# Down projection of an S5 scan plus GeGLU kernel: the h parts of more tiles ahead of the state parts in blocks 1 and 3, and other DMA numbers in its scheduler

## The chip, the cores and the metric

The kernel runs on one core of one Trainium2 chip. The metric is the device time of one execution in microseconds (us), a median over several executions. TensorE (PE in the profile) does the matmuls, VectorE (DVE) the element-wise work and the scans, ScalarE (ACT) activations and copies, GpSimd (POOL) a few small operations, and SyncE (SP) issues most of the transfers. Most executions of a kernel agree within 0.3%. The "granted clock" of a run is the mean share of full speed at which TensorE was clocked.

## The reference

The inputs are one sequence of 2048 rows with 512 columns, in bf16. Two branches read the same layer-normed rows, and the result is their sum plus the input.

```python
def _A_ref(x, ...):                       # S5: a complex diagonal state space
    Bu = jnp.einsum("bld,pd->blp", x + 0j, B_bar)
    for t in range(L):
        h = Lam_bar[None, :] * h + Bu[:, t, :]
    ...
    return 2.0 * jnp.einsum("blp,dp->bld", hseq, Cmat).real + x * Dskip

def _B_ref(x, w_gate, w_up, w_down):      # GeGLU, 512 -> 1376 -> 512
    return (_gelu(x @ w_gate) * (x @ w_up)) @ w_down

xn = _layernorm(x)
return x + _A_ref(xn, ...) + _B_ref(xn, ...)
```

The hidden product of the second branch is called h below, and the states of the first are called states. Both end in a matmul that adds to the same output tile.

## The kernel before

The rows are cut in four blocks (0 to 3) of 512 rows, each of four tiles of 128 rows. The program records every operation with what it reads and writes; a list scheduler then orders VectorE's, ScalarE's and GpSimd's work by estimated durations. TensorE and the DMA queue of SyncE keep the order in which the operations were recorded.

The estimate of a transfer is a number in one line. It places the transfer in the scheduler's mind and nothing else; a factor on the byte count stands for slow patterns:

```python
INORDER = ("tensor", "sync")
...
def dma(self, fn, nbytes, ..., queue="sync", issue=DMA_ISSUE):
    op = self._add(queue, fn, 2000.0 + nbytes / 0.30e3, "dma", reads, writes, tag, after)   # ns
...
def TR(b):                                # rows of block b, transposed, for TensorE
    for j, tt in enumerate(tts):
        S.dma(lambda e, ...: e.dma_start_transpose(XNT[b].ap[:, :, 128*j:128*(j+1)], XN[tt % 8].ap),
              3.0 * 128 * 1024, reads=[XN[tt % 8]], writes=[XTk[b][j]], tag="tr_x%d" % b, issue=1280.0)
```

The scan chain of a block runs on VectorE: four products and sums that rotate the inputs, eight scans, and four more that rotate back. The last of these (the line of the profile is L783) makes the states ready.

```python
def CHAIN(b, step=KP):
    ...
    V(... e.tensor_tensor_scan(g.ap, rb, g.ap, init, ALU.mult, ALU.add) ..., "scan")        # L767, 8 of them
    ...
    V(... e.tensor_tensor(TA.ap, ssb.ap, cos4, ALU.mult) ..., "post_c")                     # L779
    V(... e.tensor_tensor(TB.ap, ssb.ap, sin4, ALU.mult) ..., "post_s")                     # L780
    V(... e.tensor_tensor(ssb.ap[:, :, 0, :], TA..., TB..., ALU.add) ..., "post_re")        # L781
    V(... e.tensor_tensor(ssb.ap[:, :, 1, :], TB..., TA..., ALU.subtract) ..., "post_im")   # L783
```

The down projection DN(b) makes four output tiles. For each one, `seed` puts the input rows in a PSUM bank (where TensorE's sums are built up), `hidden` adds 11 matmuls over h, `states` adds 8 matmuls over the states, and `store` adds the skip term (L882) and stores the tile. The order of these on TensorE has three forms:

```python
def DN(b, split=False, tail=None):
    ...
    if split:
        for j in range(4):
            seed(j); hidden(j)
        for j in range(4):
            states(j); store(j)
    elif tail:
        for j in range(2):
            seed(j); hidden(j)
        for j in range(2):
            states(j); store(j)
        seed(2); hidden(2); states(2); store(2)
        parts = ((0, tail), (tail, D))    # the last tile in two column parts
        for c in parts:
            seed(3, *c)
        for c in parts:
            hidden(3, *c); states(3, *c); store(3, *c)
    else:
        for j in range(4):
            seed(j); hidden(j); states(j); store(j)
```

The end of the program's main part, where GU is the gate and up projection and BU the input projection of the states:

```python
        BU(2)
        CHAIN(2)
        DN(0, True)
        LN(3); SKIP(3)
        GU(2, [0, 1, 2, 10, 3, 4, 5, 6, 7]); TR(3); GU(2, [8, 9])
        BU(3)
        CHAIN(3)
        DN(1)
        GU(3, [0, 1, 2, 10, 3, 4, 5, 6, 7, 8, 9])
        DN(2)
        DN(3, tail=384)
```

## Time and profile before

| | before |
|---|---|
| time, median of 3 runs | 178.35 us (178.27 to 178.82) |
| profiled span | 176.6 us |
| TensorE's first and last matmul | from 1.02 to 174.1 us |
| states of block 1 ready / needed by TensorE | 106.6 / 108.4 us |
| states of block 3 ready / needed by TensorE | 160.9 / 162.2 us |

The first lines are from the page of the kernel before. The first gives the busy time of each engine with its share of the span and its count of instructions, the second the granted clock in 40 slices of the span.

```profile
PE 172.3 (98%) x873; PEld 84.5 (48%) x888; DVE 160.7 (91%) x283; ACT 89.5 (51%) x169; POOL 11.4 (6%) x25
...
PEclk9999999999999999999999999999999999999999
```

Two engines look full. Which one sets the time is read from the chain of work that ended last, followed back from the end and shown in order of time (start, length, what):

```profile
109.28 10.75 PE PS L864 x49
120.02 0.05 issue
120.08 2.54 PE PS L864 x11
122.62 5.18 PE PS L823 x24
127.80 1.32 PE PS L797 x16
129.12 0.05 issue
129.17 10.74 PE PS L823 x49
...
161.57 12.54 PE PS L864 x76
174.11 0.02 issue
174.13 0.29 DVE arena L882
```

It is TensorE from its first matmul on, and the only pauses are "issue" of 0.05 us. Even these are an artifact. The page counts 888 weight loads but only 873 matmuls. At 14 of the 15 such places the distance between two recorded starts is 0.432 us, exactly two matmuls of 128x512, and at the other, after a narrower one, it is 0.298 us, one narrow and one wide: one record is missing each time. Counting it, 50 matmuls of 128x512 take 10.79 us, or 215.8 ns each. The Trainium skill ("TensorE: Matmul & The Clock Gate", section "Wait — 56ns, not 53.3ns?") gives 215.7 ns from start to start once the clock is warm, and this trace agrees. So TensorE issues at its floor, with no gap, from about 6 us to the end. (The first seven matmuls, up to 3.98 us, stand 0.40 to 0.43 us apart, about half that rate, although the line PEclk has a 9 from the first slice on.)

VectorE in the timeline of the kernel before, at the start and the end of the chain of block 1 (L754, L783) and at the last chain (start, length, engine, line, operation, output and input, count, and in brackets what ended an idle time before it):

```profile
78.54 2.29 DVE L754 TENSOR_TENSOR arena<-arena 128x4096 bf16<-128x4096 bf16 x1
80.74 1.28 DVE L882 TENSOR_TENSOR arena<-PS,arena 128x512 bf16<-128x512 f32 x2
...
105.35 1.22 DVE L783 TENSOR_TENSOR arena<-arena 128x2048 bf16<-128x2048 bf16 x1
...
144.25 9.52 DVE L767 TENSOR_TENSOR_SCAN arena<-arena 128x512 bf16<-128x512 f32 x8
...
158.52 1.23 DVE L781 TENSOR_TENSOR arena<-arena 128x2048 bf16<-128x2048 bf16 x1
159.66 1.22 DVE L783 TENSOR_TENSOR arena<-arena 128x2048 bf16<-128x2048 bf16 x1
```

The chain of block 1 starts while two output adds of block 0 (L882) are still to come. The last chain ends at 159.66 + 1.22 = 160.9 us. TensorE wants these states at 162.2, found by counting the remaining matmuls back from the last one.

### The profile page before, as it was taken

The page shows a single profiled execution, that of the slowest core. Times are in us where ns is not written, and L with a number is a line of the kernel's source. Part 1 is how long each engine was busy: PE and PEld are TensorE (multiplying, and loading weights), DVE is VectorE, ACT ScalarE, POOL GpSimd, SP SyncE. Part 2 cuts the span into 40 slices and gives each one's busy share as a digit, 9 for nine tenths or more (in the row PEclk, how much of TensorE's full clock was granted, in tenths as well). Part 3 has the DMA queues.
Part 4 walks back from the last instruction along what each step waited for, and adds up shares of the span by engine and source line. Part 5 has one row for each costly group of instructions (what it writes and reads, how often), then busy time and mean ns, then how long its engine had stood idle before and what let it go on. Part 6 is the DMA issues. An engine that isn't in the chain of part 4 may idle for free.

```text
span 176.6 us, 2492 instructions
## 1 busy us (share of the span) xinstructions
PE 172.3 (98%) x873; PEld 84.5 (48%) x888; DVE 160.7 (91%) x283; ACT 89.5 (51%) x169; POOL 11.4 (6%) x25
## 2 busy tenths in 40 slices
PE   7999999999999999999999999999999999999994
PEld 2954464444544444444644444444454444444453
DVE  6979999998999979799999999899999999999811
ACT  5565678999666997003676692000767780000000
POOL 3212240200000000500000000000000000000000
PEclk9999999999999999999999999999999999999999
DMA  6997999676899000011025000100001000000311
GB/s 173 312 322 181 162 231 127 63 146 121 176 248 303 11 0 0 0 61 59 4 44 105 2 0 0 33 30 30 30 0 30 4 0 0 0 0 30 111 60 43
DMA packets 33396, 14.36 MB, mean 81 GB/s; under 512 B 23688, under 2 KB 33384, under 8 KB 33384
## 3 DMA queue, kind: packets, MB, share of 16 engines
q1 hardware_dynamic: 32944, 13.87, 35.0%
q10 hardware_dynamic: 440, 0.33, 0.6%
q8 instruction: 7, 0.11, 0.3%
q14 instruction: 5, 0.04, 0.1%
HBM read 6.46 MB, written 2.10 MB: 48 GB/s over the span
## 4 chain that ended last, share of the span: by engine, by line
PE 98%; issue 1%; DVE 0%
PE PS L864 37%; PE PS L823 32%; PE PS L734 16%; PE PS L698 7%; PE PS L797 3%; PE PS L914 2%; PE PS L673 1%; PE PS L921 0%; DVE arena L882 0%; DVE arena L479 0%; DVE arena L478 0%
## 5 line engine op out<-in xcount | busy, mean ns | idle before, releaser
L864 PE MATMUL PS<-arena 128*128 128x512 bf16 (+3 forms) x317 | 65.9, 366 | 0.3
L823 PE MATMUL PS<-arena 128*128 128x512 bf16 x258 | 57.5, 379 | 0.3
L864 PEld LDWEIGHTS PS<-arena 128*128 128x128 bf16 (+1 forms) x323 | 30.9, 98 | 35.2
L823 PEld LDWEIGHTS PS<-arena 128*128 128x128 bf16 x264 | 25.8, 98 | 30.4
L838 ACT ACTIVATE arena<-PS 128x512 bf16<-128x512 f32 x33 | 19.8, 601 | 37.5 <-PE PS L823 33.7
L767 DVE TENSOR_TENSOR_SCAN arena<-arena 128x512 bf16<-128x512 f32 x32 | 38.7, 1255 | 0.0
L734 PE MATMUL PS<-arena 128*128 128x512 bf16 x125 | 27.8, 379 | 0.2
L842 ACT ACTIVATE arena<-PS 128x512 bf16<-128x512 f32 x33 | 19.8, 598 | 5.1 <-PE PS L823 4.9
L734 PEld LDWEIGHTS PS<-arena 128*128 128x128 bf16 x128 | 12.5, 98 | 14.9
L856 ACT ACTIVATE PS<-arena 128x512 f32<-128x512 bf16 (+2 forms) x17 | 9.3, 581 | 17.5 <-DVE arena L882 17.1
L738 ACT ACTIVATE arena<-PS 128x512 bf16<-128x512 f32 x32 | 17.3, 602 | 1.3 <-PE PS L734 1.3
L882 DVE TENSOR_TENSOR arena<-PS,arena 128x512 bf16<-128x512 f32 (+2 forms) x17 | 10.8, 654 | 6.7 <-PE PS L864 6.6
L844 DVE TENSOR_TENSOR arena<-arena 128x512 bf16<-128x512 bf16 x33 | 13.2, 416 | 1.1 <-ACT arena L842 1.1
L698 PE MATMUL PS<-arena 128*128 128x192 bf16 (+2 forms) x80 | 13.0, 320 | 0.0
L624 DVE BATCH_NORM_STATS2 arena<-arena 128x6 f32<-128x512 bf16 x16 | 10.3, 686 | 0.6 <-DMA arena<-in_A_x_dram 0.6
L698 PEld LDWEIGHTS PS<-arena 128*128 128x128 bf16 x80 | 7.3, 100 | 4.7 <-issue 0.2
L756 DVE TENSOR_TENSOR arena<-arena 128x4096 bf16<-128x4096 bf16 (+1 forms) x5 | 9.2, 1861 | 0.3 <-ACT arena L620 0.3
L754 DVE TENSOR_TENSOR arena<-arena 128x4096 bf16<-128x4096 bf16 (+1 forms) x5 | 9.2, 1862 | 0.0
L780 DVE TENSOR_TENSOR arena<-arena 128x4096 bf16<-128x4096 bf16 x4 | 9.2, 2288 | 0.0
L779 DVE TENSOR_TENSOR arena<-arena 128x4096 bf16<-128x4096 bf16 x4 | 9.2, 2288 | 0.0
L707 ACT ACTIVATE arena<-PS,arena 128x192 bf16<-128x192 f32 (+1 forms) x16 | 6.6, 449 | 4.9 <-PE PS L698 4.8
L710 DVE SCALAR_TENSOR_TENSOR arena<-PS,arena 128x192 bf16<-128x192 f32 (+1 forms) x16 | 6.6, 445 | 1.4 <-ACT arena L707 1.3
(84 smaller groups left out, 112.2 us busy)
## 6 DMA issues: line engine op xcount, KB each, us to landing
out_dram<-arena SPq DMA_DIRECT2D x15, 128.0 KB, 1.7
arena<-in_A_x_dram SPq DMA_DIRECT2D x3, 512.0 KB, 5.1
arena<-in_B_w_down_dram SPq DMA_DIRECT2D x1, 1280.0 KB, 8.3
arena<-in_B_w_gate_dram SPq DMA_DIRECT2D x2, 256.0 KB, 5.1
arena<-in_B_w_up_dram SPq DMA_DIRECT2D x2, 256.0 KB, 5.4
arena<-in_B_w_gate_dram SPq DMA_DIRECT2D x1, 480.0 KB, 5.8
arena<-in_B_w_up_dram SPq DMA_DIRECT2D x1, 480.0 KB, 5.9
arena<-arena SPq DMA_TRANSPOSE x25, 2.5
```

The lines of the kernel that those rows point to most:

```text
L624: return (V(lambda e: e.bn_stats(ST[tt].ap, X[tt].ap), d_dve_1x(512), [X[tt]], [ST[tt]], "bnst"), V(lambda e: e.bn_aggr(MVt[b][j].ap, ST[t ...
L698: ins_ = e.matmul(dst, XCd(j, k), WGU[:, us[0]:us[-1] + 1, k, f0:f1], start=(k == 0), stop=(k == KD - 1))
L734: ins_ = e.matmul(PS[bank][:, :], BBT[c][dk].ap[:, 128 * s:128 * (s + 1)], XNT[b].ap[:, dk, :], start=(dk == 0), stop=(dk == KD - 1))
L738: GATE["evBu"] = ACT(lambda e, bank=bank, k3=k3, s=s, c=c: e.activation(SSc[k3][s][c].ap, PS[bank][:, :], ACTF.Copy), d_act(512), [BANK[ba ...
L767: V(lambda e, g=g, rb=rb, init=init: e.tensor_tensor_scan(g.ap, rb, g.ap, init, ALU.mult, ALU.add), d_dve_scan(512), [g, PA[RRr]] + ([CARc ...
L823: ins_ = e.matmul(PS[bank][0:m, c0:c1], W.ap[:, dk, 128 * ft:128 * ft + m], XNT[b].ap[:, dk, c0:c1], start=(dk == 0), stop=(dk == KD - 1))
L838: GATE["last_gelu"] = ACT(lambda e, bg=bg, kk=kk, m=m: e.activation(GG[kk].ap[0:m, :], PS[bg][0:m, :], ACTF.Gelu_apprx_tanh), d_act(512), ...
L842: ACT(lambda e, bu=bu, kk=kk, m=m: e.activation(UPB[kk].ap[0:m, :], PS[bu][0:m, :], ACTF.Copy), d_act(512), [BANK[bu]], [UPB[kk]], "evU")
L844: V(lambda e, kk=kk, m=m, ft=ft, k2=k2: e.tensor_tensor(HTt[k2][ft].ap[0:m, :], GG[kk].ap[0:m, :], UPB[kk].ap[0:m, :], ALU.mult), d_dve_tt ...
L856: ACT(lambda e: e.activation(PS[bank][:, c0:c1], X[tt].ap[:, c0:c1], ACTF.Copy), d_act(c1 - c0), [X[tt]], [BANK[bank]], "seed")
L864: ins_ = e.matmul(PS[bank][:, c0:c1], l_[:, 128 * j:128 * (j + 1)], r_[:, c0:c1], start=False, stop=last and n == len(ops) - 1, skip_group ...
L882: V(lambda e: e.tensor_tensor(OUTB[ko].ap[:, c0:c1], PS[bank][:, c0:c1], XD[tt].ap[:, c0:c1], ALU.add), d_dve_1x(c1 - c0), [BANK[bank], XD ...
```

## The change

The intent is to make TensorE wait less for the scan chains: more h matmuls stand ahead of the first state matmul in block 1 (four tiles, was one) and in block 3 (three tiles, was two). The scheduler also gets other DMA numbers, meant to be those of the trace.

```diff
-        op = self._add(queue, fn, 2000.0 + nbytes / 0.30e3, "dma", reads, writes, tag, after)
+        op = self._add(queue, fn, 2000.0 + nbytes / 0.35e3, "dma", reads, writes, tag, after)
... (load_T)
-                      1.2 * 512 * 1024, writes=[b_], tag="tr_" + nm, issue=3000.0)
+                      1.4 * 512 * 1024, writes=[b_], tag="tr_" + nm, issue=3000.0)
... (H0_T)
-                      3.0 * 224 * 1024, reads=[H0[j]], writes=wr, tag="tr_h0", issue=2100.0)
+                      3.5 * 224 * 1024, reads=[H0[j]], writes=wr, tag="tr_h0", issue=2100.0)
... (TR)
-                    3.0 * 128 * 1024, reads=[XN[tt % 8]], writes=[XTk[b][j]], tag="tr_x%d" % b, issue=1280.0)
+                    1.6 * 128 * 1024, reads=[XN[tt % 8]], writes=[XTk[b][j]], tag="tr_x%d" % b, issue=1280.0)
... (DN)
             elif tail:
-                for j in range(2):
+                for j in range(3):
                     seed(j); hidden(j)
-                for j in range(2):
+                for j in range(3):
                     states(j); store(j)
-                seed(2); hidden(2); states(2); store(2)
... (main part)
-        DN(1)
+        DN(1, True)
```

The factors 1.4 and 3.5 cancel the new rate, so two kinds of transfer keep their estimates. What moves is the plain transfer and the row transpose TR, whose estimate falls from 3.3 to 2.6 us (2000 ns plus 1.6 × 131072 / 350); the profile's median for on-chip transposes is 2.5 us.

## The prediction

> **What bounds the kernel.** TensorE. The page gives PE 172.3 us of the 176.6 us span (98%), VectorE 160.7 (91%), ScalarE 89.5 (51%), granted clock 1.0 of full throughout. The chain of waits is PE from 1.02 to 174.11 us, without a pause. Every 10.79 us one matmul record is missing (49 recorded), so 50 matmuls of 128x512 take 10.79 us, 215.8 ns each. The Trainium skill, "TensorE: Matmul & The Clock Gate", section "Wait — 56ns, not 53.3ns?", gives 215.7 ns as the warm start-to-start time; the trace agrees. So PE issues at its floor from about 6 us on. The groups show 0.3 us of idle time before all down-projection matmuls, 0.2 to 0.3 before the others. In the list of waits PE waits once: 1.0 us for the first memset. Outside PE's stretch: 1.0 us of start, 2.5 us of last add and store, and about 1.7 us between profiled span (176.6) and measured time.
>
> **What the change does.** It adds and removes no operation: 19 matmuls per output tile remain, with their seeds and adds. It moves state matmuls later: in block 1 the first from about 108.6 us (one tile of h parts, 2.4 us, after 106.2) to about 115.7 (four, 9.5); in block 3 from about 162.3 (two tiles after 157.6) to about 164.7 (three). On PE this reorders equal work, for zero. What is bought is slack for the scan chain: in the timeline the last state of block 1 is ready at 106.5 and that of block 3 at 160.8, so slack was 2.1 and 1.5 us and PE never waited there. The wait removed is 0.
>
> The DMA numbers change only the scheduler's idea of landing times. The DMA queue's order stays; VectorE's and ScalarE's orders change widely. Adding trace durations along VectorE's new order (estimate): the sine tables come 1.5 to 2.3 us later, the first chain runs some 3 us behind, recovering to about 1.7 by the scaling of C (about 71.0 against 73.8 needed). VectorE then stands idle for output adds of block 0, now placed ahead of the next chain, which begins near 83 us instead of 78.5. States of block 1: about 109 (needed 115.7); block 2: about 139 (needed 143.6); block 3: about 164 (needed 164.7). So the scheduler spends the new slack; PE should still not wait, but the last margin is under 1 us and my sums are good to about 1 us.
>
> **Prediction.** 178.4 us, range 177.8 to 179.3. Faster by over 2%: 1%; within 2%: 97%; slower: 2%. Nothing on the critical path is shortened; a wait before block 3's states may cost some tenths.
>
> **What would show it.** PE busy about 172.3 us, about 98%, idle before its groups still some tenths, last matmul near 174.1. VectorE's output adds of block 1 bunched near 118 to 124 us; block 3's scan chain ending 2 to 3 us later than 160.8. If my late margin is wrong, the list of waits has PE waiting for VectorE's last state combination, by under 1 us, and the last matmul ends later by the same.
>
> **What would make it wrong.** A faster result beyond 0.5% would need PE stalls in before that the trace hides, or a shorter start. A slower one: VectorE's delay reaching the gate/up product buffers or PSUM banks (ScalarE held, then PE), block 3's transposes landing after 99.3 us (they landed at 97.55), or a chain running over 1 us later than summed.

## The result, and the profile after

| | before | after |
|---|---|---|
| time, median of 6 runs | 178.40 us (178.23 to 178.82) | 178.30 us (177.97 to 178.63) |
| profiled span | 176.6 us | 177.0 us |
| last matmul ends | 174.1 us | 174.5 us |
| states of block 1 ready / needed | 106.6 / 108.4 us | 109.7 / 115.9 us |
| states of block 3 ready / needed | 160.9 / 162.2 us | 164.0 / 165.0 us |

The ratio is 0.9991, with a 95% interval of 0.9973 to 1.0009: the same time. Ratios here are the mean time of one kernel's fast runs over that of the other's of the same rounds, so not quite the ratio of the medians quoted.

The page of the changed kernel, the same lines as before:

```profile
PE 172.5 (97%) x873; PEld 84.3 (48%) x888; DVE 162.0 (92%) x283; ACT 89.9 (51%) x169; POOL 10.1 (6%) x25
...
PEclk9999999999999999999999999999999999999999
```

The chain that ended last in the changed kernel, in order of time:

```profile
2.16 5.16 DMA arena<-in_B_w_up_dram
7.37 0.50 PE PS L698 x4
...
109.65 10.75 PE PS L864 x49
120.40 0.05 issue
120.45 2.54 PE PS L864 x11
122.99 5.18 PE PS L823 x24
128.17 1.32 PE PS L797 x16
129.54 10.74 PE PS L823 x49
...
161.94 12.54 PE PS L864 x76
174.50 0.29 DVE arena L882
```

From the pieces' starts, TensorE's stretch is the same to 0.01 us. From 122.62 to 161.57 before is 38.95 us; from 122.99 to 161.94 after is 38.95 us. The whole stretch from the first matmul of GU(0) to the last one's end is 155.57 us in both. The changed kernel's profile runs 0.37 us later throughout, because its first up-projection weights landed at 7.33 us instead of 6.79 and TensorE stood for them. That may be chance: the transfer was issued at the same time (2.16 and 2.17 us), and over all the profiles its landing varies from 6.50 to 7.53 us, both ends with the old DMA numbers. The four profiles with the new numbers have 7.22 to 7.52 us, the ten with the old ones 7.10 on average, so a small effect of the numbers is not shut out. The measured times of the two kernels show none beyond their scatter.

VectorE in the changed kernel's timeline, around the output adds of block 0, at the end of the chain of block 1 and at the last chain:

```profile
75.93 0.69 DVE L882 TENSOR_TENSOR arena<-PS,arena 128x512 bf16<-128x512 f32 x1 [1.33 <-PE PS L864]
...
81.11 0.69 DVE L882 TENSOR_TENSOR arena<-PS,arena 128x512 bf16<-128x512 f32 x1
...
82.70 2.29 DVE L754 TENSOR_TENSOR arena<-arena 128x4096 bf16<-128x4096 bf16 x1
...
108.49 1.22 DVE L783 TENSOR_TENSOR arena<-arena 128x2048 bf16<-128x2048 bf16 x1
...
147.57 9.51 DVE L767 TENSOR_TENSOR_SCAN arena<-arena 128x512 bf16<-128x512 f32 x8
...
161.65 1.23 DVE L781 TENSOR_TENSOR arena<-arena 128x2048 bf16<-128x2048 bf16 x1
162.79 1.22 DVE L783 TENSOR_TENSOR arena<-arena 128x2048 bf16<-128x2048 bf16 x1
```

In the kernel before, the chain of block 1 started at 78.54 us, ahead of two of the adds. In the changed kernel, all four adds stand ahead of it and VectorE idles for them, so the chain starts at 82.70 us. Every later chain inherits some of that: the last one ends at 162.79 + 1.22 = 164.0, 3.1 us later than before. The reordering put off TensorE's need by 2.4 us (11 matmuls), plus the 0.37 us of the later start. Of block 3's slack, 1.3 us became 1.0.

So there are two statements to test: that the reordering is worth nothing in time because there was no wait to remove, and that the DMA numbers spent the slack it made.

### The profile page after: what moved, and what is told of

It reads as the page before. It is cut to its first block, busy times and chain, and to the rows that moved or that the text cites. A ratio compares the mean times of both kernels' runs of the same rounds, so it can differ in the third digit from the quotient of the medians.

```text
span 177.0 us, 2494 instructions
## 1 busy us (share of the span) xinstructions
PE 172.5 (97%) x873; PEld 84.3 (48%) x888; DVE 162.0 (92%) x283; ACT 89.9 (51%) x169; POOL 10.1 (6%) x25
## 4 chain that ended last, share of the span: by engine, by line
PE 94%; DMA 3%; SPq 1%; issue 1%; DVE 0%
PE PS L864 37%; PE PS L823 32%; PE PS L734 16%; PE PS L698 6%; PE PS L797 3%; DMA arena<-in_B_w_up_dram 3%; SPq L498 0%; PE PS L673 0%; SPq L502 0%; DVE arena L882 0%
```

## The experiments

The theory: TensorE at its issue floor sets the time as long as each block's states are ready when it wants them. The reordering moves the need and gains slack, not time; the new DMA numbers delay VectorE and spend the slack. The main rivals: the two parts each matter and cancel; VectorE, 91% busy, bounds the kernel as much as TensorE; or the DMA numbers cannot matter, as the DMA queue's order is unchanged.

All runs gave the reference's result, except for the three that are wrong on purpose. Runs of the unchanged kernel stood beside each batch; its medians were 178.2 to 178.6 us.

### The order alone (e1) and the DMA numbers alone (e2)

The edit of e1 is the second half of the change, without the DMA numbers:

```diff
-                for j in range(2):
+                for j in range(3):
                     seed(j); hidden(j)
-                for j in range(2):
+                for j in range(3):
                     states(j); store(j)
-                seed(2); hidden(2); states(2); store(2)
...
-        DN(1)
+        DN(1, True)
```

The edit of e2 is the first half alone:

```diff
-        ... 2000.0 + nbytes / 0.30e3 ...
+        ... 2000.0 + nbytes / 0.35e3 ...
-                      1.2 * 512 * 1024, ...
+                      1.4 * 512 * 1024, ...
-                      3.0 * 224 * 1024, ...
+                      3.5 * 224 * 1024, ...
-                    3.0 * 128 * 1024, ...
+                    1.6 * 128 * 1024, ...
```

> Only the reordering of the down projection (blocks 1 and 3), with the old DMA numbers. Theory (TensorE never waits, so the reordering buys slack and no time): 178.4 us, ratio to before 0.998 to 1.002; TensorE's matmul stretch unbroken; the last state combination of block 3 ready near 160.3 to 161 us and needed near 164.8, so about 4 us of slack instead of 1.5. Rival (the reordering gains, and the new DMA numbers lose it again): at least 0.5 us faster than before, with e2 slower by as much.

> Only the new DMA numbers, with the old order of the down projection. Theory: VectorE's orders move as in the changed kernel; by sums of durations the state combination of block 1 is ready near 109.2 us where TensorE needs it near 108.6, so TensorE waits about 0.6 us once, in block 1: 179.0 us, ratio 1.002 to 1.005; block 3 ready near 162.5 against a need near 163.0. Rival (the DMA numbers cannot matter since the DMA queue's order is the same): 178.4 us and no wait on TensorE. Rival (the two parts cancel): slower by 0.5 us or more, with e1 faster by as much.

Measured, with 5 rounds of runs beside the unchanged kernel: e1 178.34 us, ratio 1.0009 (0.9991 to 1.0027); e2 179.40 us, ratio 1.0063 (1.0046 to 1.0079).

In e1, the last chain is ready at 160.31 + 1.22 = 161.5 us by its timeline, where TensorE wants it at 164.7: 3.2 us of slack, and the time of before.

```profile
78.67 2.29 DVE L754 TENSOR_TENSOR arena<-arena 128x4096 bf16<-128x4096 bf16 x1
80.87 1.28 DVE L882 TENSOR_TENSOR arena<-PS,arena 128x512 bf16<-128x512 f32 x2
...
160.31 1.22 DVE L783 TENSOR_TENSOR arena<-arena 128x2048 bf16<-128x2048 bf16 x1
```

The scheduler ran anew for e1, so VectorE's order changes in it too, and its last chain is ready 0.6 us later than before; but the chain of block 1 still starts ahead of two of the adds. The trace of e1 holds all 888 matmuls, and no two starts after 6.1 us stand over 20 ns further apart than the floor, which confirms that the small pauses elsewhere are missing records.

In e2, TensorE waited. From its list of waits (engine and line, for whom, us in total, times, longest):

```profile
...
PE PS L864 <- DVE arena L783: 0.7, 1, 0.7
PE PS L698 <- DMA arena<-in_B_w_up_dram: 0.6, 1, 0.6
```

Its timeline has the chain of block 1 late, as in the changed kernel, behind all four adds, and places the first wait right after that chain's last operation:

```profile
81.30 0.69 DVE L882 TENSOR_TENSOR arena<-PS,arena 128x512 bf16<-128x512 f32 x1
...
82.23 2.29 DVE L754 TENSOR_TENSOR arena<-arena 128x4096 bf16<-128x4096 bf16 x1
...
108.53 1.22 DVE L783 TENSOR_TENSOR arena<-arena 128x2048 bf16<-128x2048 bf16 x1
...
109.80 14.22 PE L864 MATMUL PS<-arena 128*128 128x512 bf16 x65 [0.67 <-DVE arena L783]
```

The starts of the matmuls on both sides are 1.05 us apart, of which 0.22 us is one floor: 0.83 us is lost. (The list of waits counts from the modelled end of the matmul before, so it reads about 0.17 us less than the loss of issue. The needs written down before the runs were counted back from such a modelled end and are late by as much.) The theory named this wait, its place and nearly its size (0.6 us) before the run, but the ratio, 1.0063, lies above the range it gave (1.002 to 1.005). The loss in time, 1.1 us, is 0.3 us more than that wait; the late weights of the profiled run (0.6 us) show where such a rest can come from, but whether the new numbers make them later than chance does stays open.

So the parts do not cancel by one gaining and one losing. The order gains nothing by itself; the DMA numbers lose by themselves; and with both, the new order covers the loss.

### Late scans: measuring the slack (e11, e3, e4, e5, e6, e7, e12)

To measure slack directly, VectorE gets useless scans just ahead of `post_c` of block 3. They write a buffer that is overwritten later, so the result stays right. They are put in after the scheduling, so that every engine's order stays the same; the traces of e3, e4, e5, e11 and e12 show it, since VectorE, ScalarE and GpSimd run the same operations in the same order as in the traces of their kernels without the scans. e6 and e7 were rescheduled for their own order of the down projection.

```diff
         S.schedule()
+        late = [op for op in S.ops if op.tag == "post_c"][-1]
+        then = [op for op in S.ops if op.tag == "post_s"][-1]
+        post_c = late.fn
+
+        def three_scans_first(e):
+            for i in range(3):                          # 1 in e11, 6 in e12
+                e.tensor_tensor_scan(TB.ap[:, i, 0, :], PA[RRr].ap[:, 0:1].broadcast_to([128, 512]),
+                                     SSb[0].ap[:, i, 0, :], 0.0, ALU.mult, ALU.add)
+            return post_c(e)
+        late.fn = three_scans_first
+        then.deps.append(late)
         S.emit()
```

Three of them took 3.46 us in the trace of e5.

One scan on the kernel before (e11), and three (e3):

> The kernel before with one late scan (1.15 us of VectorE, less than its slack of 1.53 us at block 3). Theory: hidden, no wait on TensorE, ratio 0.998 to 1.002. Rival (any VectorE work late in the chain costs its length): plus 1.15 us, ratio 1.006.

> The kernel before, with three extra scans (about 3.55 us of VectorE) just before the last rotation of block 3; every engine's order else the same. Theory (slack of about 1.53 us at the states of block 3): TensorE waits about 2.0 us there, 180.4 us, ratio about 1.011. Rival (VectorE, 91% busy, bounds the kernel as much as TensorE): the whole 3.55 us is added, 181.9 us. Rival (VectorE is wholly hidden): no change.

Three on the order-only kernel (e4) and on the changed kernel (e5):

> The same three scans added to the kernel of e1. Theory (slack of about 4 us): no wait on TensorE, 178.4 to 178.7 us, ratio to before under 1.003. Rival (VectorE bounds): plus 3.55 us, about 181.9 us. If slack is only what it was before: 180.4 us.

> The changed kernel with the three late scans (3.55 us of VectorE before the last rotation of block 3). Theory (its slack at block 3 is 165.15 minus 164.01, about 1.1 us, since the new DMA numbers spent what the reordering gave): TensorE waits about 2.4 us there; 180.8 us where the clock stays at 1.0, up to 182.5 us in runs with a granted clock of 0.99, as seen in the run before this. Rival (the changed kernel keeps the reordering's slack): 178.4 to 178.8 us, as the order alone gave.

Three with only block 1 reordered (e6) or only block 3 (e7), both with the old DMA numbers:

> Only block 1 reordered (old DMA numbers), with the three late scans. Theory (block 1's reordering moves only the need of block 1): the need at block 3 stays at 162.4 us, TensorE waits 1.8 to 2.5 us there, 180.4 to 182.5 us. Rival (either half is enough): 178.4 to 178.8 us.

> Only block 3 reordered (old DMA numbers), with the three late scans. Theory: the need at block 3 is at 164.8 us and the chain is ready near 165.0, wait at most 0.5 us, 178.4 to 179.0 us. Rival (both halves are needed): 180.4 us or more.

| run | kernel, scans | median us (range) | ratio (95%) | wait of TensorE for L783 |
|---|---|---|---|---|
| e11 | before, 1 | 178.53 (178.30 to 178.77) | 0.9999 (0.9984 to 1.0014) | none |
| e3 | before, 3 | 181.55 (180.44 to 182.36) | 1.0179 (1.0141 to 1.0216) | 2.0 us |
| e4 | order only, 3 | 178.69 (178.25 to 178.82) | 1.0018 (0.9999 to 1.0038) | 0.2 us |
| e5 | changed, 3 | 181.90 (180.63 to 182.73) | 1.0179 (1.0118 to 1.0239) | 2.4 us |
| e6 | block 1 only, 3 | 181.24 (180.40 to 182.01) | 1.0163 (1.0116 to 1.0210) | 2.0 us |
| e7 | block 3 only, 3 | 178.76 (178.29 to 178.91) | 1.0021 (0.9996 to 1.0045) | 0.2 us |

The wait came where the theory put it each time, and with the size that it gave in e3 and e5; e4, for which it had none, waited 0.2 us. By the lists of waits:

```profile
PE PS L864 <- DVE arena L783: 2.0, 1, 2.0
```

for e3 and

```profile
PE PS L864 <- DVE arena L783: 2.4, 1, 2.4
```

for e5, and

```profile
PE PS L864 <- DVE arena L783: 0.2, 1, 0.2
```

for e4. Four things follow. One late scan costs nothing and three cost less than their length in wait, so the kernel before had a real slack between 1.1 and 3.5 us, and VectorE does not bound it. (From start to start, the matmuls of e3 lose 2.2 us at the wait, and 3.46 minus 2.2 is about the 1.3 us read from the trace before.) The order-only kernel hides nearly all of three scans. The changed kernel hides no more than the kernel before: its own DMA numbers spent the slack, which shuts out the rival that it keeps the slack of the reordering. And reordering block 1 alone buys no slack at the end (e6), while reordering block 3 alone buys all of it (e7), since the tightest need was block 3's.

A miss in size: where TensorE waited, the medians are about 1 us above wait plus 178.3, and the runs fall in two groups. In e3 they are 180.44 and 180.96 us at a granted clock of 1.0, and 182.14 and 182.36 us at 0.991. The profile of e5 fell in the second group and shows why. Busy time of each engine in five stretches around its wait; the fields that matter are PE busy with the number of matmuls, and PEclk, the granted clock:

```profile
157.00:164.90 7.90, 7.90 (x38) 3.41 (x35) 7.86 (x5) 0.00 (x0) 0.00 (x0) 1.00 0.00 0
164.90:167.40 2.50, 0.12 (x1) 0.00 (x0) 2.46 (x4) 0.00 (x0) 0.00 (x0) 1.00 0.00 0
167.40:168.50 1.10, 1.08 (x5) 0.51 (x6) 1.07 (x3) 0.00 (x0) 0.00 (x0) 1.00 0.05 15
168.50:172.20 3.70, 3.70 (x11) 1.33 (x10) 3.70 (x10) 0.28 (x1) 0.00 (x0) 0.54 0.34 116
172.20:178.00 5.80, 5.80 (x41) 3.38 (x40) 2.56 (x6) 0.00 (x0) 0.00 (x0) 1.00 0.25 85
```

1.3 us after the wait ended, the clock fell to half for some 3.4 us (matmuls 427 ns apart instead of 216), which costs about 1.7 us more. The Trainium skill ("TensorE: Matmul & The Clock Gate", section "HAM oscillation — how this bites in real kernels") describes the loss of clock after idle time. Its rule there is a gap of more than about 3.4 us; here, 6 of the 12 runs of e3, e5 and e6, with waits of 2.0 to 2.4 us in the profiled ones, have a granted clock of 0.99; of these only the one of e5 was traced. The runs of e2, e4, e7, e8, e9 and e10, with waits for L783 of at most 0.8 us in the profiled ones, all have 0.998 or more. e12 tests a longer wait:

> The order-only kernel with six late scans (6.9 us). Three gave a wait of 0.2 us, so theory: TensorE waits about 3.6 us at block 3, 182.1 us with a full clock afterwards, about 183.7 us with the half-rate stretch of some 3.4 us that the trace of the changed kernel with late scans shows after its wait. If that stretch comes by chance of where a wait of 2.0 to 2.4 us falls (6 of 12 runs had it), a longer wait should bring it more often than half of the time.

Measured: 183.74 us (183.41 to 185.10), ratio 1.0285 (1.0263 to 1.0307); the list of waits has 3.5 us; all four runs have a granted clock of 0.98 to 0.99. So the order-only kernel's slack also ends where it was put, and the longer wait lost the clock every time. In the profiled run, the matmuls were at half rate as soon as the wait ended, for about 6 us; the stretch of the wait itself already has a granted clock of 0.88. Its list of waits has

```profile
PE PS L864 <- DVE arena L783: 3.5, 1, 3.5
```

and its stretches of the wait and after it, with the same fields as above, are

```profile
164.90:168.60 3.70, 0.18 (x2) 0.01 (x1) 3.67 (x4) 0.00 (x0) 0.00 (x0) 0.88 0.00 0
168.60:174.90 6.30, 6.30 (x16) 2.29 (x17) 5.70 (x13) 0.28 (x1) 0.00 (x0) 0.53 0.27 87
```

### Less work for TensorE (e8, e9, e10)

If slack is what the reordering buys, it should show once TensorE has less to do. One of the 11 h matmuls of each output tile is left out: 16 tiles, 16 × 215.8 ns = 3.45 us. The result is wrong; the scheduler is told the old durations, so every other engine's order stays as it was.

```diff
-                ops = [(HTt[k2][ft].ap[...], WD.ap[...]) for ft in range(KF)]
+                ops = [(HTt[k2][ft].ap[...], WD.ap[...]) for ft in range(KF) if ft != 5]
...
-                PE(f, d_pe([c1 - c0] * len(ops)), ...
+                PE(f, d_pe([c1 - c0] * (len(ops) + (not last))), ...
```

> Wrong result on purpose: the kernel before with one of the 11 h matmuls of every output tile left out (16 tiles, 3.45 us of TensorE), every engine's order else the same. Theory (TensorE's issue rate is the bound until the scan chain of block 3 is late): the need at block 3 comes 14 matmuls (3.0 us) earlier, at 159.4 us, against readiness near 160.7; TensorE waits 1.0 to 1.5 us; 175.9 to 176.6 us instead of 174.9. Rival (VectorE bounds): no gain at all, 178.3 us. Rival (only TensorE counts): 174.9 us.

> Wrong result on purpose: the order-only kernel of e1 with the same 16 matmuls left out. Theory: the need at block 3 comes 15 matmuls (3.24 us) earlier, about 161.5 us, just when the chain is ready (161.53), so TensorE waits at most 0.3 us and nearly the whole 3.45 us shows: 174.9 to 175.3 us. Rival (slack is worth nothing, since TensorE is the bound in all three): the same time as the kernel before with the 16 left out.

> Wrong result on purpose: the changed kernel with the same 16 matmuls left out. Theory: the need at block 3 comes at 161.9 us, the chain is ready near 163.2 to 164, TensorE waits 1.3 to 2.1 us: 176.2 to 177.0 us. Rival (the changed kernel keeps the reordering's slack): 174.9 to 175.3 us.

| run | kernel with 16 matmuls fewer | median us (range) | ratio (95%) | wait for L783 |
|---|---|---|---|---|
| e8 | before | 175.54 (175.09 to 175.75) | 0.9841 (0.9817 to 0.9865) | 0.3 us |
| e9 | order only | 175.06 (174.56 to 175.26) | 0.9816 (0.9795 to 0.9837) | none |
| e10 | changed | 176.02 (175.62 to 176.09) | 0.9869 (0.9848 to 0.9890) | 0.8 us |

Without a wait, taking away TensorE work takes away time nearly one for one (e9: 178.28 of its batch minus 175.06 is 3.2 of 3.45 us), which settles that TensorE is the bound; a VectorE bound would have left 178.3 us. The expectations of e8 and e10 were missed by 0.4 and 0.2 us, on the fast side. The error was one term: the chain was taken to be ready when it had been, but in e8 it was ready at 158.74 + 1.22 = 160.0 us, not 160.7, because VectorE stands idle for less time ahead of its output adds when TensorE's tiles come earlier (in the changed kernel 2.1 us between the chains of block 0 and block 3, in e10 0.9 us). The ranking is as expected: the order-only kernel gets nearly all of it, the changed kernel, in the same batch, 1.0 us less. The distance from e8 to e9 is smaller, and the two ran in different batches, so it is not leaned on.

No version here beats both kernels with the right result: e1 has the most slack and the same time.

## Why the prediction was right

- *TensorE is the bound and is at its floor.* Right: the stretch is 155.57 us in both, and e8 to e10 show time following its work.
- *The reordering removes a wait of 0 and buys slack.* Right: e1 is 1.0009, and e4 against e3 shows the slack in time.
- *The DMA numbers change only orders on VectorE and ScalarE, and delay the chains.* Right: the chain of block 1 starts at 82.70 us ("near 83"), states are ready at 109.7, 138.8 and 164.0 us ("about 109, 139, 164").
- *The last margin is under 1 us.* Measured 1.0 us; TensorE did not wait. The prediction called its own sums good to about 1 us, no finer than this margin, so that TensorE did not wait is in part luck.
- *Slack before the change of 2.1 us in block 1 and 1.5 us in block 3.* By the starts of the matmuls 1.8 and 1.3 us; the prediction had counted from a modelled end.
- *The first chain recovers to 1.7 us behind by the scaling of C, ready at about 71.0.* Off by 0.8 us: that work ended at 69.07 + 2.73 = 71.8 us. It stayed off the critical path.
- *Adds of block 1 bunched at 118 to 124 us.* Right: they start at 117.92, 119.91, 121.68 and 123.46 us.
- Not foreseen: the row transposes of block 1, of which the last landed at 31.87 us, where TensorE wanted them near 32.1. That margin was 1.1 us before and 0.2 after. The prediction summed VectorE's chains and did not look there; a worse turn of the schedule could have cost time in a place that it never checked.

## What to carry to other kernels

Before moving work to shorten a wait, find the wait on the bounding engine; where there is none, the move can only buy slack, and slack is worth time only when something later uses it up. Where a list scheduler decides orders, its duration numbers are a change of their own: run them apart from the edit, since here they alone cost 0.6% and the edit hid that. Slack can be measured by adding useless work after scheduling, so that no order moves, until the bounding engine starts to wait.

## What the Trainium skill lacked or had wrong

- "TensorE: Matmul & The Clock Gate", sections "HAM oscillation — how this bites in real kernels" and "🎯 Why this matters for your kernels", allow idle gaps of TensorE up to about 3.4 or 3 us. Here waits of 2.0 to 2.4 us went with a lower granted clock in 6 of 12 runs; in the one of these that was traced, half rate for about 3.4 us beginning 1.3 us after the wait, about 1.7 us lost. After a wait of 3.5 us it was 4 of 4 runs.
- "Perfetto Trace Analysis", section "Identifying the Most-Contended Engine", names the busy share of weight loads, with MFU, as the measure of how far TensorE is from its limit. Here that share is 48% while 128x512 matmuls follow each other at 215.8 ns, the floor; the distance from start to start told it, the weight loads' share did not. (MFU was not worked out here.)
- No page that was consulted says that matmul records can be missing at regular distance. Here about one of 50 was missing in 4 of 14 traces (in the kernels before and after, 873 recorded of 888), and each looks like a pause of 0.05 us on the chain of waits; the other ten traces, of nearly the same programs, held all.
